# Row starts of x's two parts and of the feed-forward buffers at staggered byte offsets modulo 512

## The chip, the cores and the metric

The kernel runs on one core of a Trainium2 chip. The metric is the device time of one execution in microseconds. The engines are named as in the profile: PE (matmul) with PEld (its weight loads), DVE (vector), ACT (scalar), POOL (GpSimd) and SP, whose queue issues the DMAs.

## What is computed

Linear attention with exponential features (8 batches, 8 heads, 576 tokens, head size 64, 128 features), whose output, 4608 tokens by 512, goes through a two-layer feed-forward block with softplus between the layers (512 to 2048 to 512):

```python
def phi(x):                                   # x: q or k, scaled by 1/sqrt(sqrt(D))
    proj = np.einsum('bhsd,md->bhsm', x, omega)
    h = proj - np.sum(x * x, axis=-1, keepdims=True) / 2.0
    h = h - np.max(h, axis=-1, keepdims=True)
    return np.exp(h) / np.sqrt(m)
kv = np.einsum('bhsm,bhsd->bhmd', phi(k), v)
num = np.einsum('bhsm,bhmd->bhsd', phi(q), kv)
den = np.einsum('bhsm,bhm->bhs', phi(q), phi(k).sum(axis=2))[..., None] + 1e-06
x = (num / den).transpose(0, 2, 1, 3).reshape(B * S, H * D)
h = x @ w_in
out = (np.maximum(h, 0.0) + np.log1p(np.exp(-np.abs(h)))) @ w_out
```

## The kernel before

**Number form.** The feed-forward matmuls take fp32r operands (a rounded 4-byte form). To keep the precision, each operand is held as two parts, a high one (a copy rounded to fp32r) and a low one (the remainder). A product is three matmuls: high by high, high by low, low by high.

**x.** xh and xl are the two parts of x, transposed: 128 partitions by NCC = 4 rows of RING = 1024 tokens, 4 bytes each. A row's index is the block of 128 of the 512 columns of x; the 1024 token places are a ring that is reused as the token blocks pass. They are written by DVE or ACT from PSUM (x_high at L720 and L879, x_low at L747 and L885, and plan_rest at L1018 and L1021 for the last block) and read by PE as the moving operand of layer 1.

**The feed-forward block.** Tokens are taken in two blocks of 256 and eight of 512 (blocks_of), and for each the 16 chunks of d_ff (NFC) in turn (plan_step, L913). For a chunk, layer1 (L917) runs 12 matmuls into one PSUM bank h: for each of four rows cc it streams xh against wh (L923), xl against wh (L924) and xh against wl (L925). ACT takes the magnitude, the exponential and the logarithm into u (L929, L932, L935), DVE adds max(h, 0) (L938), ACT or DVE makes gh, the rounded copy of u (L942), and DVE or POOL makes gl, the remainder (L946). layer2 (L948) then takes gh and gl as the weights of the matmuls, 128 tokens at a time, and streams the 512 columns of w2 (L952 to L954) into an accumulator that is kept for all 16 chunks. u, gh and gl have two buffers each, in the pool ff. The weights' two parts stay in SBUF for the whole run, as w1[fc] and w2[fc] (tiles wi and wo), 2 by 512 columns each.

**Order.** The order of all instructions on each engine is worked out by a planner (in_order, L91) from costs and due times that are constants in the source, before any is issued; the tiles of a kind that has several buffers are handed out there too. Attention work of the next batch is spread between the feed-forward matmuls (L399, L424 are its projections, L563 and L664 its key sums, L865 its outputs). L1103 is a filler matmul of the first stage.

**Where tiles lie.** A pool takes its place in SBUF when its tiles are known, in the order of the pools: const, at, ff. Within a pool each tile follows the last one. Of one tile, the bytes of a row of one partition follow each other, so that the row xh[:, cc] begins 4 x RING = 4096 bytes after the row before. PSUM places are not touched by any of this.

```python
xh = const.tile([P, NCC, RING], F32R, name="xh")
xl = const.tile([P, NCC, RING], F32R, name="xl")
...
nc.tensor.matmul(b["h"], wh, xh[:, cc, t], start=cc == 0, stop=False)
nc.tensor.matmul(b["h"], wh, xl[:, cc, t], start=False, stop=False)
nc.tensor.matmul(b["h"], wl, xh[:, cc, t], start=False, stop=cc == NCC - 1)
...
nc.tensor.matmul(acc[tt], gh, w2[fc][:, 0], start=fc == 0, stop=False)
nc.tensor.matmul(acc[tt], gh, w2[fc][:, 1], start=False, stop=False)
nc.tensor.matmul(acc[tt], gl, w2[fc][:, 0], start=False, stop=fc == NFC - 1)
```

Of the kernel before, what the change touches and what calls it, by code (L numbers as in the profile page):

```python
# [11 lines left out]
F32R = mybir.dt.float32r  # L12
# [7 lines left out]
P = 128  # L20
# [7 lines left out]
NCC = DM // P  # L28
TB = 512
RING = 2 * TB  # L30
# [157 lines left out]
def favor_softplus_kernel(ctx, tc, q0, k0, qx, kx, tx, vv, om, wi, wo, out):  # L188
# [5 lines left out]
            name=nc.get_next_instruction_name(), act_func_set_id=ACT_SET_LN_EXP,  # L194
# [3 lines left out]

    const = ctx.enter_context(tc.tile_pool(name="const", bufs=1))
    at = ctx.enter_context(tc.tile_pool(name="at", bufs=1))  # L200
    ff = ctx.enter_context(tc.tile_pool(name="ff", bufs=2))
    dram = ctx.enter_context(tc.tile_pool(name="dram", bufs=2, space=bass.MemoryType.DRAM))
    ps = ctx.enter_context(tc.tile_pool(name="ps", bufs=8, space=PSUM))
# [10 lines left out]

    marks = const.tile([P, 16], F32, name="marks")
    junk = const.tile([P, 1, M], BF16, name="junk")
    xh = const.tile([P, NCC, RING], F32R, name="xh")
    xl = const.tile([P, NCC, RING], F32R, name="xl")
    rest = dram.tile([P, NCC, B * D], F32, name="rest", tag="rest", bufs=1)


# [1 line left out]
    f = ff.tile([P, 512], F32, name="omf1", tag="t2.0", bufs=1)[:, :M]  # L223
# [689 lines left out]
    def plan_step(i, t0, n, fc, due, acc, box):  # L913
        nm = f"_{i}_{fc}"
        b = {}
# [22 lines left out]
            nc.vector.scalar_tensor_tensor(b["u"], b["h"], 0.0, b["u"], ALU.max, ALU.add)  # L938

        def high(e):  # L940
            b["gh"] = ff.tile([P, TB], F32R, name=f"gh{nm}", tag="gh" + b["gs"], bufs=1)[:, :n]
            (nc.scalar.copy if e == "ACT" else nc.vector.tensor_copy)(b["gh"], b["u"])  # L942

        def low(e):
# [21 lines left out]
        s = do("ACT", act(n), due - 54.43, log, after=[s])  # L966
        p = do("DVE", dve(n), due - 54.63, plus, after=[s], give=[(b, "hs")])
        h = do(("DVE", "ACT"), (dve(n, 2), act(n)), due + 11.74, high, after=[p], take=[("g", b, "gs")], port=True)
        l = do(("DVE", "POOL"), (dve(n), pool(n)), due + 8.00, low, after=[h], give=[(b, "us")], port=True)
        box["l1"], ends = a, []  # L970
# [240 lines left out]
```

## Time and profile before

| what | value |
|---|---|
| median of 3 runs | 1017.37 us |
| lowest and highest | 1016.28, 1018.88 us |
| the profiled execution's own time | 1014.9 us |
| its span, first to last instruction | 1013.1 us |
| granted PE clock, mean | 0.998 |
| busy share of PE, PEld, DVE, ACT, POOL | 99%, 80%, 73%, 65%, 12% |

The profile is of one execution. Its page has the busy time of each engine, the chain of work that ended last, followed back from the last instruction, and the groups of instructions by source line. A group's row reads: line, engine, operation, output <- inputs, partitions x elements, count, then busy us and mean ns of one, then the idle us of the engine just before them and what ended it. A row of waits reads: who waited <- for whom: us in total, times, longest. A row of the timeline reads: start us, length us, engine, line, operation, count. PE's lengths overlap, since matmuls are pipelined; the distance of two starts does not.

### The profile page before, as it was taken

What the parts mean: (1) busy time and instruction counts of PE and PEld (TensorE: products, weight loads), DVE (VectorE), ACT (ScalarE), POOL (GpSimd) and SP (SyncE); (2) the same over time, 40 slices, a digit from 0 to 9 for tenths busy, and PEclk for the clock granted to TensorE, in tenths of its full rate; (3) what the DMA queues carried; (4) which work ended last, traced back from release to release, by engine and by line L of the source; (5) the groups of instructions that cost most, each with busy time, mean ns of one, the idle gap of its engine ahead of it and who ended that gap; (6) DMA issues with size and microseconds to landing.
All of it is one profiled execution on the core that took longest, in us unless ns stands there. A gap on an engine that the chain in (4) does not pass through costs nothing.

```text
span 1013.1 us, 17023 instructions
## 1 busy us (share of the span) xinstructions
PE 998.3 (99%) x5752; PEld 809.0 (80%) x5752; DVE 742.7 (73%) x2027; ACT 659.7 (65%) x1592; POOL 119.1 (12%) x125
## 2 busy tenths in 40 slices
PE   9999999999999999999999999999999999999997
PEld 8888788877777787878787777778788778888885
DVE  6999988988888787878787887878797733222222
ACT  6999977767666675756576666667575645444442
POOL 2212221010021010110112011211011100000000
PEclk9999999999999999999999999999999999999999
DMA  9774344433442424343333333352533121001001
GB/s 345 305 265 176 116 151 126 150 114 101 121 145 72 133 84 141 115 128 97 120 126 102 113 94 110 96 149 73 152 115 89 54 75 54 1 1 42 1 1 42
DMA packets 64175, 113.82 MB, mean 112 GB/s; under 512 B 18236, under 2 KB 36824, under 8 KB 64088
## 3 DMA queue, kind: packets, MB, share of 16 engines
q1 hardware_dynamic: 64088, 112.73, 35.0%
q8 instruction: 46, 0.75, 0.3%
q14 instruction: 41, 0.34, 0.1%
HBM read 85.68 MB, written 27.03 MB: 111 GB/s over the span
## 4 chain that ended last, share of the span: by engine, by line
PE 87%; DVE 6%; ACT 4%; DMA 2%; issue 1%; POOL 0%; SPq 0%; DVEq 0%
PE acc L952 13%; PE h L923 12%; PE acc L953 12%; PE acc L954 12%; PE h L924 12%; PE h L925 12%; PE ppk L399 3%; PE xp L865 3%; PE kt L563 3%; PE ppq L424 2%; DMA xk<-kx 1%; DVE junk L785 1%; PE fill L1103 1%; DMA xq<-qx 1%; ACT xq L469 0%
## 5 line engine op out<-in xcount | busy, mean ns | idle before, releaser
L923 PE MATMUL h<-xh,wi 128*128 128x512 f32 (+1 forms) x640 | 239.5, 374 | 1.4 <-DVE u L938 1.4
L924 PE MATMUL h<-xl,wi 128*128 128x512 f32 (+1 forms) x640 | 236.0, 369 | 0.0
L925 PE MATMUL h<-xh,wi 128*128 128x512 f32 (+1 forms) x640 | 235.6, 368 | 0.0
L952 PE MATMUL acc<-wo,gh 128*128 128x512 f32 x576 | 231.1, 401 | 0.5 <-ACT kvs L581 0.5
L953 PE MATMUL acc<-wo,gh 128*128 128x512 f32 x576 | 225.4, 391 | 0.0
L954 PE MATMUL acc<-wo,gl 128*128 128x512 f32 x576 | 224.8, 390 | 0.2 <-DVE gl L946 0.2
L929 ACT ACTIVATE u<-h 128x512 f32<-128x512 f32 (+1 forms) x160 | 89.2, 558 | 168.2 <-PE h L925 160.1
L938 DVE SCALAR_TENSOR_TENSOR u<-h,u 128x512 f32<-128x512 f32 (+1 forms) x160 | 101.2, 633 | 119.5 <-ACT u L935 117.7
L923 PEld LDWEIGHTS h<-xh,wi 128*128 128x128 f32 x640 | 120.5, 188 | 29.6 <-issue 5.4
L925 PEld LDWEIGHTS h<-xh,wi 128*128 128x128 f32 x640 | 120.5, 188 | 20.6
L924 PEld LDWEIGHTS h<-xl,wi 128*128 128x128 f32 x640 | 120.5, 188 | 19.0
L952 PEld LDWEIGHTS acc<-wo,gh 128*128 128x128 f32 x576 | 108.1, 188 | 29.9 <-issue 7.2
L954 PEld LDWEIGHTS acc<-wo,gl 128*128 128x128 f32 x576 | 108.1, 188 | 24.1 <-DVE gl L946 0.6
L953 PEld LDWEIGHTS acc<-wo,gh 128*128 128x128 f32 x576 | 108.4, 188 | 18.0
L942 ACT CAST gh<-u 128x512 fp32r<-128x512 f32 (+1 forms) x122 | 71.4, 585 | 57.1 <-PE acc L953 52.7
L946 DVE TENSOR_TENSOR gl<-u,gh 128x512 fp32r<-128x512 f32 (+1 forms) x128 | 85.4, 667 | 26.2 <-ACT gh L942 24.7
L935 ACT ACTIVATE u<-u 128x512 f32<-128x512 f32 (+1 forms) x160 | 94.4, 590 | 4.8
L932 ACT ACTIVATE u<-u 128x512 f32<-128x512 f32 (+1 forms) x160 | 94.6, 591 | 3.9
L785 DVE CUSTOM_DVE_ANT_0 junk<-phq,zb 128x128 bf16<-128x128 f32 (+1 forms) x228 | 79.1, 347 | 17.6 <-ACT phq L446 1.7
L794 POOL TENSOR_TENSOR phq<-phq,dnq 128x512 f32<-128x512 f32 (+1 forms) x43 | 45.9, 1071 | 209.9 <-DVE dnq L790 129.8
L946 POOL TENSOR_TENSOR gl<-u,gh 128x512 fp32r<-128x512 f32 (+1 forms) x32 | 36.2, 1130 | 280.9 <-ACT gh L942 148.3
L469 ACT ACTIVATE phk<-ppk,smk 128x128 f32<-128x128 f32 x230 | 63.8, 377 | 2.6 <-DVE smk L461 1.3
(129 smaller groups left out, 1293.3 us busy)
## 6 DMA issues: line engine op xcount, KB each, us to landing
xk<-kx SPq DMA_DIRECT2D x28, 512.0 KB
xq<-qx SPq DMA_DIRECT2D x28, 512.0 KB
fdq<-flq SPq DMA_DIRECT2D x28, 512.0 KB
qq<-fdq SPq DMA_DIRECT2D x112, 128.0 KB
rawi<-wi SPq DMA_DIRECT2D x16, 512.0 KB
rawo<-wo SPq DMA_DIRECT2D x16, 512.0 KB
out<-o SPq DMA_DIRECT2D x32, 256.0 KB
v<-vv SPq DMA_DIRECT2D x14, 576.0 KB
```

The lines of the kernel that those rows point to most:

```text
L785: nc.vector.tensor_tensor_reduce(jk[r, c % jk.shape[1]], ph[r, c], q.zb[r, h], 1.0, 1e-6, ALU.mult, ALU.add, dn[r, 0, c : c + 1])
L923: nc.tensor.matmul(b["h"], wh, xh[:, cc, t], start=cc == 0, stop=False)
L924: nc.tensor.matmul(b["h"], wh, xl[:, cc, t], start=False, stop=False)
L925: nc.tensor.matmul(b["h"], wl, xh[:, cc, t], start=False, stop=cc == NCC - 1)
L929: nc.scalar.activation(b["u"], b["h"], AF.Abs)
L932: nc.scalar.activation(b["u"], b["u"], AF.Exp, scale=-1.0)
L935: nc.scalar.activation(b["u"], b["u"], AF.Ln, bias=1.0)
L938: nc.vector.scalar_tensor_tensor(b["u"], b["h"], 0.0, b["u"], ALU.max, ALU.add)
L946: (nc.vector if e == "DVE" else nc.gpsimd).tensor_tensor(b["gl"], b["u"], b["gh"].bitcast(F32), ALU.subtract)
L952: nc.tensor.matmul(acc[tt], gh, w2[fc][:, 0], start=fc == 0, stop=False)
L953: nc.tensor.matmul(acc[tt], gh, w2[fc][:, 1], start=False, stop=False)
L954: nc.tensor.matmul(acc[tt], gl, w2[fc][:, 0], start=False, stop=fc == NFC - 1)
```

## The change

xh and xl move from the pool const to a pool of their own, xs, which is opened between at and ff, and their rows become 4 and 8 elements longer (16 and 32 bytes). gh's two buffers become 8 elements (32 bytes) longer, which moves gl and what follows in the pool ff. The added elements are neither written nor read.

```diff
     const = ctx.enter_context(tc.tile_pool(name="const", bufs=1))
     at = ctx.enter_context(tc.tile_pool(name="at", bufs=1))
+    xs = ctx.enter_context(tc.tile_pool(name="xs", bufs=1))
     ff = ctx.enter_context(tc.tile_pool(name="ff", bufs=2))
...
-    xh = const.tile([P, NCC, RING], F32R, name="xh")
-    xl = const.tile([P, NCC, RING], F32R, name="xl")
+    xh = xs.tile([P, NCC, RING + 4], F32R, name="xh")
+    xl = xs.tile([P, NCC, RING + 8], F32R, name="xl")
...
         def high(e):
-            b["gh"] = ff.tile([P, TB], F32R, name=f"gh{nm}", tag="gh" + b["gs"], bufs=1)[:, :n]
+            b["gh"] = ff.tile([P, TB + 8], F32R, name=f"gh{nm}", tag="gh" + b["gs"], bufs=1)[:, :n]
```

The starts of rows and buffers, in bytes from the start of a partition (modulo 512 in brackets), as they follow from the tiles' sizes:

| tile | before | after |
|---|---|---|
| xh, rows 0 to 3 | 1216 + 4096 cc (192 each) | 179904 + 4112 cc (192, 208, 224, 240) |
| xl, rows 0 to 3 | 17600 + 4096 cc (192 each) | 196352 + 4128 cc (256, 288, 320, 352) |
| u, two buffers | 214720, 220864 (192) | 214912, 221088 (384, 416) |
| gh, two buffers | 216768, 222912 (192) | 216960, 223136 (384, 416) |
| gl, two buffers | 218816, 224960 (192) | 219040, 225216 (416, 448) |
| o, two buffers | 212672, 227008 (192) | 212864, 227264 (384, 448) |
| omf, omr, the weights, all attention tiles | as they were | 32768 lower (the same modulo 512) |

## The prediction

> **What bounds the kernel now.** I read the page's head and its chain first, then PE's waits, then stretches of the timeline with and without company on the other engines.
>
> ```profile
> span 1013.1 us, 17023 instructions
> PE 998.3 (99%) x5752; PEld 809.0 (80%) x5752; DVE 742.7 (73%) x2027; ACT 659.7 (65%) x1592; POOL 119.1 (12%) x125
> ...
> PE 87%; DVE 6%; ACT 4%; DMA 2%; issue 1%; POOL 0%; SPq 0%; DVEq 0%
> ```
>
> The matmul queue is never out of work. What it waited for, longest first (8 pairs, 7.2 us in all; the first two and the last are shown):
>
> ```profile
> PE ppq L424 <- DVE spq L417: 1.5, 2, 1.2
> PE h L923 <- DVE u L938: 1.4, 2, 0.7
> ...
> PE acc L954 <- DVE gl L946: 0.2, 1, 0.2
> ```
>
> So no producer sets the time: the number of matmuls and the step from one to the next do. Most are the feed-forward ones, three lines in each layer; one line of each stands here with its count by shape (the two others of a layer have the same counts):
>
> ```profile
> L952 PE MATMUL acc<-wo,gh 128*128 128x512 f32 x576 | 231.1, 401 | 0.5 <-ACT kvs L581 0.5
> L923 PE MATMUL h<-xh,wi 128*128 128x512 f32 x512 | 201.9, 394 | 0.0
> ...
> L923 PE MATMUL h<-xh,wi 128*128 128x256 f32 x128 | 37.7, 294 | 1.4 <-DVE u L938 1.4
> ```
>
> That is 3 x 576 + 3 x 512 = 3264 matmuls of 512 columns and 3 x 128 = 384 of 256. Their modelled durations overlap, so the step is read from starts. Timeline of PE, two rows of a quiet stretch near the end (ten steps apart), and two rows of a stretch of 256-column matmuls (eight steps apart):
>
> ```profile
> 949.64 0.39 PE L923 MATMUL h<-xh,wi 128*128 128x512 f32 x1
> ...
> 951.91 0.39 PE L953 MATMUL acc<-wo,gh 128*128 128x512 f32 x1
> ```
>
> ```profile
> 99.83 0.28 PE L923 MATMUL h<-xh,wi 128*128 128x256 f32 x1
> ...
> 100.79 0.28 PE L925 MATMUL h<-xh,wi 128*128 128x256 f32 x1
> ```
>
> 2.27 us over ten steps is 227 ns for 512 columns; 0.96 us over eight is 120 ns for 256. The difference, 107 ns for 256 columns, is 0.417 ns a column, and what is left of either step is a fixed **13.3 ns**. The feed-forward work is 3264 x 0.227 + 384 x 0.120 = 787 us of the span's 1013.1; a change that leaves the counts alone must alter these steps, or it alters nothing.
>
> **The change, part by part.** No instruction is added, taken away or moved: on every engine the same operations stand in the same order with the same waits, and no shape that an engine sees is different. Only addresses differ. Added up from the tile sizes, every row of xh and xl, and u, gh, gl, the o tiles of the feed-forward pool and the weights, begins at 192 modulo 512 before. After, the four rows of xh begin at 192, 208, 224 and 240, those of xl at 256, 288, 320 and 352; the two sets of u are at 384 and 416, of gh at 384 and 416, of gl at 416 and 448, the o tiles at 384 and 448. The weights and all attention tiles move down by 32768 bytes as a block and keep their places modulo 512. So three things could change in time: what engines lose to each other in SBUF, what PE's own two reads (moving operand and weights) lose to each other, and what an operand loses by beginning off a round address.
>
> *Losses between engines.* Two stretches of 12 us, a crowded one and a quiet one:
>
> ```profile
> 732.00:744.00 12.00, 12.00 (x54) 9.95 (x53) 11.37 (x33) 9.98 (x22) 2.08 (x2) 1.00 0.35 122
> ...
> 950.00:962.00 12.00, 12.00 (x55) 9.93 (x54) 3.05 (x5) 4.97 (x8) 0.00 (x0) 1.00 0.00 0
> ```
>
> After the times stand PE, PEld, DVE, ACT and POOL (busy us, count), granted clock, DMA share and GB/s. In the first DVE is busy for 11.37 us, ACT for 9.98, and DMA runs; in the second DVE is at 3.05, ACT at 4.97 and DMA at nothing. PE's steps in the crowded one, 54 of them between these two rows:
>
> ```profile
> 732.02 0.39 PE L925 MATMUL h<-xh,wi 128*128 128x512 f32 x1
> ...
> 744.26 0.39 PE L954 MATMUL acc<-wo,gl 128*128 128x512 f32 x1
> ```
>
> 12.24 us over 54 is 226.7 ns, the quiet step. The rows resolve 10 ns in 54 steps, 0.2 ns a step, so for matmuls inside a long run the whole loss is at most 3264 x 0.2 = 0.7 us. The Trainium skill, SBUF — State Buffer, section "Who interferes with whom", says that PE and ACT never wait on anyone there and that only the pair of ports shared by VectorE and GpSimd is contended; by that rule, too, addresses cost PE nothing, and these rows agree. Just after a switch from attention work, though, the steps are longer:
>
> ```profile
> 787.23 0.40 PE L954 MATMUL acc<-wo,gl 128*128 128x512 f32 x1
> ...
> 788.16 0.40 PE L424 MATMUL ppq<-omr,spq 128*128 128x256 f32 x2
> ```
>
> Four steps, 0.93 us: 232.5 ns, 5.8 above. If that were losses in SBUF and all of it went, what would it be worth? The attention groups that cut the runs:
>
> ```profile
> L399 PE MATMUL ppk<-omf,xk 64*128 64x128 f32 x532 | 40.4, 287 | 1.5 <-DMA xk<-kx 1.2
> ...
> L424 PE MATMUL ppq<-omr,spq 128*128 128x256 f32 x194 | 35.7, 285 | 1.5 <-DVE spq L417 1.5
> ```
>
> With two L424 or sixteen L399 to a group that is about 130 switches; five steps each at 5.8 ns is 3.8 us, an estimate. I take **0**, bounds -4.5 (these 3.8 and the 0.7 above) and 0: the bumps follow the switch and not the company, since run 732 to 744 has the company without them.
>
> The other engines, by the same test. DVE's and ACT's costliest operations in the crowded stage 300 to 800, and in the quiet one from 880 on (minimum, median, maximum in ns):
>
> ```profile
> L938 DVE SCALAR_TENSOR_TENSOR u<-h,u x74: 651/691/694, 301.8 to 798.8; 128x512 f32<-128x512 f32 x74
> L932 ACT ACTIVATE u<-u x74: 617/632/655, 299.9 to 797.4; 128x512 f32<-128x512 f32 x74
> ```
>
> ```profile
> L938 DVE SCALAR_TENSOR_TENSOR u<-h,u x20: 691/692/693, 883.1 to 986.5; 128x512 f32<-128x512 f32 x20
> L932 ACT ACTIVATE u<-u x20: 632/632/645, 881.8 to 985.1; 128x512 f32<-128x512 f32 x20
> ```
>
> 691 against 692 and 632 against 632: nothing to win. What they could lose is one mode: gh is copied by DVE in some cases at twice its usual rate.
>
> ```profile
> L942 DVE CAST gh<-u x38: 253/417/1116, 58.9 to 793.8; 128x512 fp32r<-128x512 f32 x27, 128x256 fp32r<-128x256 f32 x11
> ```
>
> If the new start of gh's second buffer lost that rate, such a cast would cost about what L938 does, 691 instead of 417 ns: 274 x 38 = 10.4 us of DVE over the whole span. DVE is idle for 27% of it and PE waited 0.2 us in all for gl, which comes behind that cast, so I cost it at **0**. The cover is that slack; without it half the casts (those of one buffer) would be on the path, +5 us.
>
> *PE's two reads.* The weights of the next matmul are loaded while a matmul streams:
>
> ```profile
> 949.87 0.39 PE L924 MATMUL h<-xl,wi 128*128 128x512 f32 x1
> 949.87 0.19 PEld L925 LDWEIGHTS h<-xh,wi 128*128 128x128 f32 x1
> ```
>
> Before, both reads begin at 192 modulo 512. Whether the fixed 13.3 ns are the price of that, no row shows, as no row has matmuls of this type from other residues. The nearest are f32 matmuls of the first stage, with groups of n rows merged (start, length, count):
>
> ```profile
> 42.64 1.03 PE L701 MATMUL tpq<-ident,xq 128*128 128x128 f32 x8
> ...
> 47.93 1.11 PE L714 MATMUL nuq<-kvs,xq 128*128 128x65 f32 x8
> ...
> 49.10 0.61 PE L1103 MATMUL fill<-ident 128*128 128x128 f32 x4
> ```
>
> Less the modelled 0.27 us of the last one, a step is 0.76/7 = 0.109 us for L701 (ident at 384, weights at 192), 0.84/7 = 0.120 for L714 (kvs at 64 and steps of 260 bytes, weights at 192; its first step is longer than the rest) and 0.34/3 = 0.113 for L1103 (both operands at the same address). The same address on both sides thus costs 4 ns at most against L701, and less than nothing against L714. I take **0**; the lower bound is the whole 13.3 ns of every matmul whose residues part: layer 1 keeps 192 against 192 for two of twelve (xh's first row), so 1920 x 10/12 = 1600, and all 1728 of layer 2, where gh and gl leave 192: 3328 x 13.3 = -44 us.
>
> *Round addresses.* 192 is a multiple of 64. After, rows 2 to 4 of xh and rows 2 and 4 of xl begin 16, 32 or 48 bytes past one: 8 of the 12 matmuls of each layer-1 group. L714 above has such starts (260-byte steps) at 0.120 us or less, no more than 11 ns above L701, but at a slower rate of columns. If a 64-byte piece had to be read once more, its 16 columns at 0.417 ns would be 6.7 ns a matmul: 1920 x 8/12 = 1280 of them, **+8.5 us**. I take 0, the nearer value by L714, and keep the 8.5.
>
> **The sum.** 0 + 0 + 0 on the profiled execution's 1014.9 us (span 1013.1 and 1.8 around it). The median of the runs is 1017.37, 2.5 more, so in terms of the median the forecast is 1017.4 us, and 1016.3 to 1018.9 if the new runs spread as the old ones did. About 0.3%, 3 us, is what a measurement of this kernel can tell from no change.
>
> **Rivals.**
> *The bumps go* (-4.5): losses between engines were behind the longer steps after a switch, and staggering ends them: 1017.4 - 4.5 = 1012.9. For it: the bumps are real. Against: crowded runs without any.
>
> *The fixed step goes* (-44): PE's two reads collide because both start at 192, and parted residues end it: 973 us. For it: the 13.3 ns are the same for 256 and 512 columns, as a loss per weight load would be; L1103 stands 4 ns above L701. Against: L714, and that two reads which advance at different rates would meet at other places as well. The Trainium skill, TensorE: Matmul & The Clock Gate, section "Back-to-back issue gap", gives N/2.4 + 2.5 ns, 215.8 for 512 columns, as the isolated gap; the trace's 227 is 11 above it, and by that rule a stream without the loss would save an estimated 37 us on these 3328. No run here shows which it is.
>
> *Off-round rows cost a piece* (+8.5): each layer-1 matmul whose row is off a multiple of 64 bytes takes 6.7 ns more, 1026 us. It decides at once, since PE has no slack to hide it: any cost above 2.4 ns on the 1280 passes the 3 us. For it: no row of this matmul type begins off 64. Against: L714's starts.
>
> *The change does not do what it says*: two of the twelve pairs of layer 1 keep 192 on both sides, and the weights are not moved. That only shrinks the others and gives 1017.4 again.
>
> **Chances.** No change 0.68 (with the last rival), the bumps 0.10, the fixed step 0.08, off-round rows 0.14. The range leaves out only the fixed step: 1012 to 1026. Of the bumps' 0.10, 0.09 lies below the 0.3% line; faster 0.17, within 0.69, slower 0.14.
>
> **What would show it.** Right: 226.7 ns steps between feed-forward matmuls in 732 to 744 and near 950, 120 ns for 256 columns, medians of 691 for L938 and 632 for L932, and DVE's L942 at 417. The first rival shows in steps after a switch at 227; the second in a step under 227 at 950, equal for both widths; the third in L923 to L925 longer than L952 to L954, with L924 split by row. A fixed step that hangs on addresses is what would make this forecast wrong by most.

## The result and the profile after

Five runs each. Before: 1017.37 us median (1016.28 to 1018.88). After: 1025.79 us median (1025.23 to 1030.98). The ratio is 1.0092 with a 95% interval of 1.0066 to 1.0118: slower by 8.4 us. The profiled execution of the changed kernel took 1025.75 us, its span 1024.0 us; that is 10.9 us more than the profiled span of before, whose execution was 2.5 us quicker than the median.

The head of the changed kernel's page, and its waits of PE (7 pairs, the first and the last shown):

```profile
span 1024.0 us, 17023 instructions
PE 1009.1 (99%) x5752; PEld 808.0 (79%) x5752; DVE 742.1 (72%) x2027; ACT 660.2 (64%) x1592; POOL 118.8 (12%) x125
...
PE 89%; DVE 6%; DMA 2%; ACT 1%; issue 1%; SPq 0%; DVEq 0%; ACTq 0%
```

```profile
PE ppk L400 <- DMA xk<-kx: 1.6, 2, 0.9
...
PE acc L953 <- ACT kvs L582: 0.5, 1, 0.5
```

PE is as full as it was, no new wait of any size stands there, and DVE and ACT were busy for as long as before to within 1 us. Their costliest operations in the crowded stage, 300 to 800 (source lines are one higher than before):

```profile
L939 DVE SCALAR_TENSOR_TENSOR u<-h,u x73: 652/691/693, 299.6 to 795.6; 128x512 f32<-128x512 f32 x73
L933 ACT ACTIVATE u<-u x72: 629/632/654, 300.7 to 793.5; 128x512 f32<-128x512 f32 x72
L943 DVE CAST gh<-u x18: 410/418/426, 301.4 to 752.2; 128x512 fp32r<-128x512 f32 x18
```

Medians of 691, 632 and 418 ns: these operations kept their times. What grew is PE's own step. Near the end, where the feed-forward work is alone, one chunk of d_ff is 12 matmuls of layer 1 and 12 of layer 2. The first matmuls of these groups in the timeline, two chunks of before and two of after:

```profile
845.60 0.39 PE L923 MATMUL h<-xh,wi 128*128 128x512 f32 x1
848.32 0.39 PE L952 MATMUL acc<-wo,gh 128*128 128x512 f32 x1
...
856.48 0.39 PE L923 MATMUL h<-xh,wi 128*128 128x512 f32 x1
```

```profile
847.37 0.39 PE L924 MATMUL h<-xh,wi 128*128 128x512 f32 x1
850.16 0.39 PE L953 MATMUL acc<-wo,gh 128*128 128x512 f32 x1
852.96 0.39 PE L924 MATMUL h<-xh,wi 128*128 128x512 f32 x1
855.72 0.39 PE L953 MATMUL acc<-wo,gh 128*128 128x512 f32 x1
858.49 0.39 PE L924 MATMUL h<-xh,wi 128*128 128x512 f32 x1
```

48 steps took 10.88 us before (226.7 ns each) and take 11.12 us now (231.7): 5.0 ns more, in layer 1 (2.79 and 2.76 us for 12, against 2.72) and in layer 2 (2.80 and 2.77). From one chunk to the next the values alternate, as the two sets of u, gh and gl do.

Where in the run the 10.9 us of span were lost is seen at the last attention output in the chain, which has the same place in both programs:

```profile
821.83 1.23 PE xp L865 x8
```

```profile
828.74 1.23 PE xp L866 x8
```

It starts 6.9 us later; from there to the end it is 191.3 us before and 195.3 after, 4.0 more. The loss is spread over the whole feed-forward work and does not need the other engines' company.

It is not 5.0 ns on every one of the 3264 steps, though, which would be 16 us. Worked out from every start of the two traces: the times from a feed-forward matmul of 512 columns to PE's next start grew by 8.0 us ahead of that output (2457 of them) and by 4.0 us behind it, 12.0 in all, while the rest of PE's work came out 1.1 us shorter. In 200 to 800 the first twelve feed-forward steps after a switch from attention work, which were long already, went from 230.2 to 231.9 ns on the mean; the later ones went from 226.7 to 231.6.

### The profile page after: what moved, and what is told of

It is laid out like the page before. It is cut to its first block, busy times and chain, and to the rows that moved or that the text cites. A ratio compares the mean times of both kernels' runs of the same rounds, so it can differ in the third digit from the quotient of the medians.

```text
span 1024.0 us, 17023 instructions
## 1 busy us (share of the span) xinstructions
PE 1009.1 (99%) x5752; PEld 808.0 (79%) x5752; DVE 742.1 (72%) x2027; ACT 660.2 (64%) x1592; POOL 118.8 (12%) x125
## 4 chain that ended last, share of the span: by engine, by line
PE 89%; DVE 6%; DMA 2%; ACT 1%; issue 1%; SPq 0%; DVEq 0%; ACTq 0%
PE acc L953 13%; PE h L924 13%; PE acc L954 12%; PE h L925 12%; PE h L926 12%; PE acc L955 12%; PE ppk L400 3%; PE xp L866 3%; PE kt L564 3%; PE ppq L425 2%; DMA xk<-kx 1%; DVE junk L786 1%; PE fill L1104 1%; DVE smq L450 1%; DMA xq<-qx 1%
## 5 line engine op out<-in xcount | busy, mean ns | idle before, releaser
L955 PE MATMUL acc<-wo,gl 128*128 128x512 f32 x576 | 227.2, 394 | 0.0
```

## The experiments

The theories at the start: **A**, PE's step depends on the distance between the places where its weight load and its moving operand begin; **B**, the rival of the prediction, an operand's own start off a multiple of 64 bytes costs; **C**, x's new place in SBUF costs, whatever its residues.

### Parts alone, the move alone, a common shift

The edits of e1, e2 and e3 are shown against the changed kernel. e1_ff_only has the change's feed-forward buffers and x at 192:

```diff
-    xh = xs.tile([P, NCC, RING + 4], F32R, name="xh")
-    xl = xs.tile([P, NCC, RING + 8], F32R, name="xl")
+    xh = xs.tile([P, NCC, RING], F32R, name="xh")
+    xl = xs.tile([P, NCC, RING], F32R, name="xl")
+    xs.tile([P, 48], F32, name="gap")
```

> Undoes x's part: xh and xl keep rows at 192 modulo 512, u, gh and gl stand as in the change. Theory A (what counts is the distance between where the weight load and the moving operand begin): only steps that load gh or gl are longer, by about 5 ns on 512 columns, layer-1 steps stay at 227; the time is about +4 to +5 us on before. Theory B (what counts is an operand's own start off a multiple of 64 bytes, as predicted for x's rows): gh's first buffer at 384 costs nothing, those at 416 something; under +3 us. Theory C (what counts is that x lies elsewhere in SBUF): all steps longer, +8 us.

Measured: 1.0063 of before (1.0046 to 1.0080). Two chunks:

```profile
845.65 0.39 PE L925 MATMUL h<-xh,wi 128*128 128x512 f32 x1
848.38 0.39 PE L954 MATMUL acc<-wo,gh 128*128 128x512 f32 x1
851.18 0.39 PE L925 MATMUL h<-xh,wi 128*128 128x512 f32 x1
853.92 0.39 PE L954 MATMUL acc<-wo,gh 128*128 128x512 f32 x1
856.70 0.39 PE L925 MATMUL h<-xh,wi 128*128 128x512 f32 x1
```

Layer 2 takes 2.80 and 2.78 us (233 and 232 ns a step), layer 1 2.73 and 2.74 (227.5 and 228). In layer 2 the moving operand, w2, has not changed its place modulo 512; only the weights, gh and gl, have. B does not fit: in the chunks with gh at 384, a multiple of 64, only the four matmuls with gl at 416 start off one, which at 6.7 ns each would be 2 ns a step on the mean, and both kinds of chunk are 5 to 7 ns a step slower.

e2_x_only has the change's rows of x and the feed-forward buffers at 192; the pool xs stands behind ff and gh is as long as before:

```diff
-    xs = ctx.enter_context(tc.tile_pool(name="xs", bufs=1))
     ff = ctx.enter_context(tc.tile_pool(name="ff", bufs=2))
+    xs = ctx.enter_context(tc.tile_pool(name="xs", bufs=1))
...
-            b["gh"] = ff.tile([P, TB + 8], F32R, name=f"gh{nm}", tag="gh" + b["gs"], bufs=1)[:, :n]
+            b["gh"] = ff.tile([P, TB], F32R, name=f"gh{nm}", tag="gh" + b["gs"], bufs=1)[:, :n]
```

> Undoes the feed-forward buffers' part: u, gh, gl and o at 192 modulo 512, x's rows at the changed starts, with their pool behind the feed-forward pool. Theory A: only layer-1 steps are longer, about +4 to +5 us on before, layer-2 steps stay at 227. Theory B: layer-1 steps whose row begins off 64 bytes are longer, the others not; up to +8.5 us. Theory C: all steps longer, +8 us.

Measured: 1.0078 (1.0059 to 1.0098).

```profile
847.86 0.39 PE L924 MATMUL h<-xh,wi 128*128 128x512 f32 x1
850.64 0.39 PE L953 MATMUL acc<-wo,gh 128*128 128x512 f32 x1
853.40 0.39 PE L924 MATMUL h<-xh,wi 128*128 128x512 f32 x1
```

Layer 1 is at 2.78 us (232 ns a step), but layer 2, whose two reads both begin at 192, is at 2.76 (230). No theory had that; the sweep below accounts for it. Nor do the parts add up: 0.6% and 0.8% alone, 0.9% together.

e3_moved has the new pool and none of the added elements:

```diff
-    xh = xs.tile([P, NCC, RING + 4], F32R, name="xh")
-    xl = xs.tile([P, NCC, RING + 8], F32R, name="xl")
+    xh = xs.tile([P, NCC, RING], F32R, name="xh")
+    xl = xs.tile([P, NCC, RING], F32R, name="xl")
...
-            b["gh"] = ff.tile([P, TB + 8], F32R, name=f"gh{nm}", tag="gh" + b["gs"], bufs=1)[:, :n]
+            b["gh"] = ff.tile([P, TB], F32R, name=f"gh{nm}", tag="gh" + b["gs"], bufs=1)[:, :n]
```

> The new pool alone, without any of the added elements: x lies above the attention tiles and everything begins at 192 modulo 512 again. Theories A and B: steps of 227 ns, time as before within 0.3%. Theory C: steps of 231 to 232 ns and +8 us.

Measured: 0.9996 (0.9986 to 1.0006), and the steps of before:

```profile
847.53 0.39 PE L924 MATMUL h<-xh,wi 128*128 128x512 f32 x1
850.25 0.39 PE L953 MATMUL acc<-wo,gh 128*128 128x512 f32 x1
852.97 0.39 PE L924 MATMUL h<-xh,wi 128*128 128x512 f32 x1
```

12 steps in 2.72 us in both layers. C falls.

e4_common32 is before with one small tile longer. The 16 bytes more move all that follows by 32, since tiles are placed at multiples of 32 bytes:

```diff
-    marks = const.tile([P, 16], F32, name="marks")
+    marks = const.tile([P, 20], F32, name="marks")
```

> Before, with one small tile of the first pool four elements longer, so that x, the weights, the attention tiles and the feed-forward buffers all begin at 224 modulo 512: 32 bytes off a multiple of 64, but both reads of PE still alike. Theory A: steps of 227 ns, time as before within 0.3%. Theory B: all 1920 layer-1 matmuls off 64 bytes, 6.7 ns each, +13 us. Theory C: as before.

Measured: 0.9992 (0.9979 to 1.0006).

```profile
846.54 0.39 PE L923 MATMUL h<-xh,wi 128*128 128x512 f32 x1
849.26 0.39 PE L952 MATMUL acc<-wo,gh 128*128 128x512 f32 x1
851.98 0.39 PE L923 MATMUL h<-xh,wi 128*128 128x512 f32 x1
```

Every operand of the feed-forward matmuls begins 32 bytes off a multiple of 64, and the steps are 2.72 us for 12. B falls; A stands: what counts is where the two operands stand to each other, as far as one common shift can show it.

### One distance for all of x

In these kernels all rows of xh and xl stand the same number of bytes past the weights' place modulo 512, and layer 2 is as before. The pool xs stands behind ff as in e2; N is the distance in bytes:

```diff
-    xh = xs.tile([P, NCC, RING + 4], F32R, name="xh")
-    xl = xs.tile([P, NCC, RING + 8], F32R, name="xl")
+    xs.tile([P, N // 4], F32, name="gap")
+    xh = xs.tile([P, NCC, RING], F32R, name="xh")
+    xl = xs.tile([P, NCC, RING], F32R, name="xl")
```

For 4, 8, 16, 240 and 248 bytes, which are not multiples of 32, xh and xl are the two halves of one tile that is read from N bytes on. Each was run once. The expectations, in the order 32, 64, 128, 256, 16, 96, 192, 224, 4, 8, 248, 240 bytes:

> All rows of xh and xl 32 bytes past the weights' place modulo 512 (224 against 192), layer 2 as before (192 against 192). Theory A1 (any distance between the two reads' starts costs): layer-1 steps of 229 to 237 ns, layer-2 steps near 227. Theory A2 (only a distance that differs from one matmul to the next costs): 227 in both layers. A third (some distances are cheaper than none): layer-1 steps under 227.

> As x_by_32, with 64 bytes (256 against 192). A1: layer-1 steps of 229 to 237 ns. A2: 227. A third: under 227.

> As x_by_32, with 128 bytes (320 against 192). A1: layer-1 steps of 229 to 237 ns. A2: 227. A third: under 227.

> As x_by_32, with 256 bytes (448 against 192), half of the modulus. A1: layer-1 steps of 229 to 237 ns. A2: 227. A third: under 227; if the pattern repeats after 256 bytes, 227 as well.

> All rows of xh and xl 16 bytes past the weights' place (208 against 192), the smallest distance that the change has. If any distance that is not a multiple of 256 costs: layer-1 steps of 229 ns or more and +3 to +10 us. If 16 bytes are within one access of the memory: 227 and no change.

> Distance 96 bytes. If any distance that is not a multiple of 256 costs: layer-1 steps of 229 to 237 ns, layer-2 steps 1 to 3 ns above before, +3 to +10 us. If some distances are cheaper than none: under 227 and under 1014 us.

> Distance 192 bytes, with a period of 256 the same as 64 bytes the other way. If the loss hangs on the distance alone and not on which read is ahead: about as x_by_64, 229 to 232 ns. If the read that is ahead matters: another value, perhaps under 227.

> Distance 224 bytes, with a period of 256 the same as 32 bytes the other way. If it hangs on the distance alone: about as x_by_32, 232 to 234 ns and +8 to +10 us. If the read that is ahead matters: another value, perhaps under 227.

> Rows of xh and xl 4 bytes, one element, past the weights' place (196 against 192). If the distance counts in pieces of 16 bytes or more, what is crossed is a piece's border once in four elements: 227 or a small loss. If each element counts: 229 ns or more in layer 1. If the fixed 13.3 ns are a collision of equal starts: under 227.

> 8 bytes past (200 against 192). In pieces of 16 bytes or more: 227 or a small loss; each element: 229 ns or more; a collision of equal starts: under 227.

> 248 bytes past, with the period of 256 the same as 8 bytes ahead (440 against 192). As x_by_8 if only the size of the distance counts; another value if it matters which read is ahead; a collision of equal starts: under 227.

> 240 bytes past, the same as 16 bytes ahead (432 against 192). As x_by_16 (about 231.5 ns in layer 1, 229 in layer 2 near the end) if only the size of the distance counts; another value if it matters which read is ahead; a collision of equal starts: under 227.

The lengths of a group of 12 in one chunk near 850, each the difference of two starts in the timeline, with the step worked out from it; the time beside the one run of before on the same chip. Those single runs of before differ by 3.5 us, so the steps carry the argument and not the times:

| distance | layer 1, us for 12 | ns a step | layer 2, us for 12 | ns a step | time, us | before there |
|---|---|---|---|---|---|---|
| 0 (before) | 2.72 | 226.7 | 2.72 | 226.7 | | |
| 4 | 2.84 | 236.7 | 2.73 | 227.5 | 1030.88 | 1017.68 |
| 8 | 2.80 | 233.3 | 2.75 | 229.2 | 1029.33 | 1017.68 |
| 16 | 2.78 | 231.7 | 2.75 | 229.2 | 1026.90 | 1021.22 |
| 32 | 2.81 | 234.2 | 2.75 | 229.2 | 1027.27 | 1019.36 |
| 64 | 2.76 | 230.0 | 2.77 | 230.8 | 1022.11 | 1019.36 |
| 96 | 2.82 | 235.0 | 2.75 | 229.2 | 1028.08 | 1021.22 |
| 128 | 2.79 | 232.5 | 2.74 | 228.3 | 1025.40 | 1019.36 |
| 192 | 2.80 | 233.3 | 2.74 | 228.3 | 1026.01 | 1021.22 |
| 224 | 2.80 | 233.3 | 2.74 | 228.3 | 1026.69 | 1021.22 |
| 240 | 2.80 | 233.3 | 2.72 | 226.7 | 1026.26 | 1017.68 |
| 248 | 2.81 | 234.2 | 2.73 | 227.5 | 1027.63 | 1017.68 |
| 256 | 2.72 | 226.7 | 2.72 | 226.7 | 1016.28 | 1019.36 |

Every distance but 256 makes these steps of layer 1 longer, by 3 to 10 ns, and 256 is the same as 0: for 512 columns A1 (any distance costs) holds. That it repeats every 256 bytes rests on 256 itself; nothing beyond it was tried. A2 (only a distance that changes from row to row costs) falls, since all rows of layer 1 have one distance here. Nothing is under 226.7, so no distance tried beats before in these steps. The order of the operands matters little in three pairs (32 and 224, 16 and 240, 8 and 248 lie within 2 ns of each other), but 192 is 3 ns above 64, which has the same size the other way.

The matmuls of 256 columns, in the first two token blocks, do not follow this rule. Two rows twenty steps apart, in the same place of the program, from before and from x_by_192:

```profile
85.14 0.28 PE L923 MATMUL h<-xh,wi 128*128 128x256 f32 x1
...
87.53 0.28 PE L925 MATMUL h<-xh,wi 128*128 128x256 f32 x1
```

```profile
85.20 0.28 PE L925 MATMUL h<-xh,wi 128*128 128x256 f32 x1
...
87.47 0.28 PE L927 MATMUL h<-xh,wi 128*128 128x256 f32 x1
```

2.39 us is 119.5 ns a step at equal starts, 2.27 us is 113.5 at a distance of 192: here the distance makes the step shorter. On the mean of all such stretches of a trace, from the fifth step on, it is 119.7 ns before, 118.4 after the change, 117.1 at 32 bytes, 117.4 at 64, 115.4 at 192 and 122.0 at 4; before, e3, e4 and x_by_256, all with equal starts, agree within 0.2. So in these kernels the sign of the effect is not the same for the two widths. Only 384 of the 3648 feed-forward matmuls are this short, and the kernel as a whole loses.

From PE's timeline of one of these kernels, x_by_32, back at 512 columns, the starts of layer 1, of layer 2, of layer 2's seventh matmul and of the next layer 1:

```profile
849.05 0.40 PE L925 MATMUL h<-xh,wi 128*128 128x512 f32 x1
851.86 0.40 PE L954 MATMUL acc<-wo,gh 128*128 128x512 f32 x1
...
853.25 0.39 PE L954 MATMUL acc<-wo,gh 128*128 128x512 f32 x1
...
854.61 0.40 PE L925 MATMUL h<-xh,wi 128*128 128x512 f32 x1
```

Layer 2 has equal starts here. Its first six steps take 1.39 us (231.7 ns each), its last six 1.36 (226.7). So matmuls with equal starts fall back to the short step, but only after some of them, here about six; a layer behind one with a distance pays for that too. Averaged over the unbroken chunks of a trace it is five steps behind a distance of 192 and ten behind 64. This is the 230 ns of layer 2 in e2, and it is why the parts do not add up: with x or the weights of layer 2 displaced alone, each chunk pays for one layer's distance and for the other's way back; with both displaced no whole layer is on its way back. The same averages bear it out. Over 226.9 ns before, e1 has 1.1 ns a step in layer 1 and 5.6 in layer 2, e2 has 5.1 and 3.4, the change 4.5 and 5.4: without the two ways back (1.1 and 3.4) the parts make 10.7, near the change's 9.9. No run shows the way back by itself.

## Why the prediction was wrong

*What bounds the kernel* was right: PE's steps set the time, no producer does, and the change acted through those steps. The growth of the 512-column ones, 12.0 us by the two traces, covers the span's 10.9.

*Losses between engines* were right at 0: DVE and ACT kept 691 and 632 ns, the steps after a switch did not get shorter, and the loss a step is largest at the end, where the other engines have little to do. The cast by DVE kept its rate (418 ns).

*PE's two reads* is the step that failed. I took 0 with a bound on one side only, -44 us: equal starts were weighed as a possible cost, never as what keeps the step at 226.7 ns. The term cost 8.4 us by the medians. For 512 columns the runs show the reverse sign: 0 and 256 give the short step, all else 3 to 10 ns more. Only the 256-column matmuls did what the second rival hoped for, and by 4 ns on the mean at best (115.4 at 192), not 13.3; a fixed step that is the same for both widths, as the prediction had read it, there is not. Its count was off as well: if 256 counts as 0, gl's second buffer at 448 is still equal to w2's place, so the places of 3040 matmuls parted and not of 3328. Two arguments misled there. One was that reads which advance at different rates would meet in other places as well, so the start could not matter; the sweep shows that it does, and x_by_32 that its effect takes some matmuls to settle. The other was reading the f32 matmuls (L701, L714, L1103) for the fp32r ones: with steps of 109 to 120 ns for at most 128 columns they were no measure of matmuls at one column per 0.417 ns. The prediction's last line named the right spot all the same: a fixed step that hangs on addresses.

Of the page on SBUF that the prediction drew on (the Trainium skill, SBUF — State Buffer, "Who interferes with whom"), the measurement agrees with the part on other engines. That PE never waits it does not confirm: the page has the reads of the moving operand and of the weights as two independent ports, and here a matmul of 512 columns took 3 to 10 ns longer by the places of the two operands alone. That the two reads hold each other up is the likely reading, but argued: PEld's own busy time stayed the same (809.0 and 808.0 us), and no trace shows where in the step the time goes.

*Round addresses*, the rival on the slow side, gave 1026 us, and 1025.8 came, just inside the range of 1012 to 1026. That is luck: its mechanism predicted layer 1 alone, and e4, with every feed-forward operand 32 bytes off a multiple of 64, costs nothing.

The signs named at the end of the prediction served: steps over 226.7 ns near 850 in both layers, with 691 and 632 ns on DVE and ACT, say at once that it is neither x's rows alone nor the other engines.

## What to carry to other kernels

Where PE streams matmuls that each load new weights, and its step is the bound, compare the byte addresses of the two operands modulo 256 before moving or padding a tile: for 512 columns equal places were the best of thirteen distances, and losing them cost 0.6 to 0.9% in the three kernels that were run several times. Measure it for each width: at 256 columns seven of the eleven unequal distances gained 1 to 4 ns a step. Staggering buffers against conflicts needs a conflict that the trace shows; equal operation times in crowded and quiet stages say there is none. And an unknown cost wants a bound on both sides, above all where everything stands alike before and the trace has no row of the other case.

## What the runs showed of the hardware that was not expected

The step of an fp32r matmul of 512 columns with new weights was 226.7 ns when weights and moving operand began at the same place modulo 256 bytes, and 230 to 237 ns otherwise, one element (4 bytes) already giving 236.7. At 256 columns it was 119.7 ns at equal starts and between 115.4 (192 bytes) and 122.0 (4 bytes) otherwise. After a stretch with a distance, matmuls of 512 columns with equal starts needed five to ten steps to be back at 226.7. Why this is so is open: what lies behind the 256 bytes, and why the shorter matmuls gain, was not measured. Open too is whether the longer steps just after a switch from attention work, seen before the change, are the same settling; that was not tried. In x_by_4, x_by_8 and x_by_248 the rows also begin off a multiple of 16 bytes, and no run separates that from the distance.
